# Eight late steps of a tail's down-projection: split float32r products replaced by plain float32 products on two array tiles

## Chip, cores and metric

One Trainium2 chip (trn2), one of its cores. The time is device microseconds of that core, the median of several runs; the trace is one profiled execution.

## What is computed

Block-sparse attention feeds a two-layer feed-forward block. The change touches only the second matrix product of the feed-forward block, `g @ w_out`.

```python
def _attn_ref(q, k, v, sampled_blocks):          # B,H,S,D = 4,8,768,64; blocks of 32
    ...
    return np.matmul(attn, v).astype(np.float32)

def _moe_ref(x, w_in, w_out):                    # x 3072x512, w_in 512x2048, w_out 2048x512
    h = x @ w_in
    g = h * (1.0 / (1.0 + np.exp(-1.702 * h)))
    return (g @ w_out).astype(np.float32)
```

## The kernel before

The 3072 tokens are cut into `NC` = 6 chunks of `CT` = 512 tokens, and the 2048 hidden features into `NF` = 16 groups of 128. A step m = 16 c + f is chunk c and feature group f, so there are 96 steps, 0 to 95. A step has an up product (`h`, 128 features x 512 tokens), a gate (`g`) and a down product, which adds `g`'s 128 features times 128 rows of `w_out` (128 x 512) to four PSUM banks of 128 tokens each.

Every float32 operand of the two products is split into a high part rounded to float32r and a low part (the float32 value minus the high part, again float32r). A product is then three matmuls: high x high, high x low, low x high. For the down product that means, for each step:

- `gate_hi` (line 594, ScalarE) casts `g` to `ghi`, `gate_lo` (line 602, VectorE) subtracts to get `glo`.
- `stream` (line 557) starts a DMA on the SP queue that brings one 256 KB row block of `w_out` from a DRAM scratch tensor into a tile `wst` (pool `work`, two buffers); `split` (line 562 on ScalarE, line 563 on VectorE) makes its high and low part in one of three `wout` buffers.
- `down(m, 0)` issues eight matmuls of 128x128 weights (the tokens of `ghi`) against 512 moving columns (lines 625 and 626: `wout` high, `wout` low, for each of the four banks), and `down(m, 1)` the four of `glo` (line 621). So a step is 12 matmuls over 512 columns.

`slot(d, part)` runs `down(d, part)` and after part 1 `split(d + 2)` and `stream(d + 4)`: weights are fetched four steps ahead and split two steps ahead. [...]

The last two chunks are computed as one block product with fewer multiplications (`pair`, line 837's matmuls), which leaves the gate results of chunk 5 as plain float32 in a resident tile `gs` (16 x 512 columns). The helper tile `snap` (pool `tail`, four buffers) takes copies of PSUM banks there and is last used by the eighth `pair`. After the eighth `pair`, `last` runs steps 78 to 95 with nothing else beside them: for each step of chunk 5 a `gate_hi`, `gate_lo` one step ahead, then the two parts of `slot`. Step 95 is the last of its chunk: it orders its 12 matmuls bank by bank, so that `store` can empty each bank (lines 660 and 662) while the next one is finished.

The attention at the start uses plain float32 matmuls on parts of the array (`tile_position`): the values of the dense blocks (line 419) as two tiles of 128 rows x 64 columns over 65 moving columns, the scores as 64x64 tiles over 384 columns (line 342, four tiles) and as 64x32 tiles over 256 columns (line 332, eight tiles). A call of line 419 issues 24 matmuls in the code, with the two tiles alternating.

Of the kernel before, what the change touches and what calls it, by code (L numbers as in the profile page):

```python
# [9 lines left out]
F32 = mybir.dt.float32  # L10
# [8 lines left out]
P = 128  # L19
# [5 lines left out]
DM = H * D  # L25
DF = 2048
NCT = DM // P
NF = DF // P
NU = (NB - 2) // 2
UT = 2 * BLK  # L30
CU = 8
CT = CU * UT
NC = B * S // CT
NN = CT // P
# [8 lines left out]
MAIN = (NC - TAIL) * NF  # L43
FREEQ = QT * (MAIN - NF) - 10
SPARE = (7, 1, 2, 0)
DV = D + 1
VROW = H * DV
NK = S // P
VDROW = 4 * NK * DV
SV = S + BLK  # L50
# [4 lines left out]
class Kernel:  # L55
# [205 lines left out]
    def load_v(self, e):  # L261
        nc, b, u, r = self.nc, e["b"], e["u"], e["at"]
        if u is None:
            flat = self.vown[r].rearrange("p j c -> p (j c)")[:, 0:VDROW]
            nc.sync.dma_start(out=flat, in_=self.vd[b, e["i"]])
            e["vd"] = flat.rearrange("p (h k a d) -> p h k a d", h=2, a=2, d=DV)
            return
# [126 lines left out]
    def values(self, g):  # L394
# [4 lines left out]
        if g["first"]:  # L399
            un["av"] = self.bank[self.psum("a", un["n"])[0]]  # L400
        sums = un["av"][:, 0:NPAIR * DV].rearrange("p (k d) -> p k d", d=DV)
        if self.sparse(g):
            for i in range(2):
                for h in range(2):
                    for k in range(2):
                        for c in range(4):
                            a, j = c // 2, c % 2
                            at = VROW * (un["b"] % 2) + DV * (2 * (2 * i + a) + h)
                            src = self.vown[r][:, j] if k == j else self.vmid[r]
                            nc.tensor.matmul(  # L410
                                sums[BLK * c:BLK * (c + 1), 2 * i + h], g["pt"][h][:, 2 * i + k, BLK * c:BLK * (c + 1)],
                                src[:, at:at + DV], start=(k == 0), stop=(k == 1), tile_position=(0, BLK * c), skip_group_check=True)
        else:
# [43 lines left out]
    def weights(self):  # L457
# [55 lines left out]
        for k, (f, i) in enumerate(todo):  # L513
            while i == 1 and f - WRING > self.downs - 1:
                yield
            fetch(k + 2)
            if i == 0 and f == NWIN:
                self.opening.close()
                late = self.pool("late", 1)
                self.win += [late.tile([P, 2 * DM], F32R, name=f"win{n}") for n in range(NWIN, NF)]  # L520
            if "a" not in tiles[k]:
                self.flush()
            raw, a = tiles[k]["raw"], tiles[k]["a"]
            nc.vector.tensor_scalar(out=a, in0=a, scalar1=3, scalar2=None, op0=ALU.logical_shift_left)
            yield
            nc.vector.scalar_tensor_tensor(out=a, in0=raw[:, :, 1], scalar=-0x80000000, in1=a, op0=ALU.bitwise_and,
                                           op1=ALU.bitwise_or)
            first(k + 1)
            yield
            if k > 0:  # L530
                if "high" not in tiles[k - 1]:
                    self.flush()
                last(k - 1)
            yield
            nc.vector.scalar_tensor_tensor(out=a, in0=raw[:, :, 0], scalar=29, in1=a, op0=ALU.logical_shift_right,
                                           op1=ALU.bitwise_or)
            tiles[k]["t"] = self.win[f] if i == 0 else self.wout[f % WRING]
            high(k)
            yield
        self.flush()  # L540
        last(len(todo) - 1)

    def flush(self):
# [9 lines left out]
    def stream(self, m):  # L553

        if NF <= m < NC * NF:
            self.wst[m] = self.work.tile([P, DM], F32, name="wst")
            self.nc.sync.dma_start(out=self.wst[m], in_=self.ws[m % NF])

    def split(self, m):
        if m in self.wst:  # L560
            w, t = self.wst.pop(m), self.wout[m % WRING]
            self.nc.scalar.copy(out=t[:, 0:DM], in_=w)  # L562
            self.nc.vector.tensor_tensor(out=t[:, DM:2 * DM], in0=w, in1=t[:, 0:DM].bitcast(F32), op=ALU.subtract)  # L563
# [41 lines left out]
    def down(self, m, part):  # L605
        nc = self.nc
        if m < 0:
            return
        c, f = divmod(m, NF)
        if c == 0:  # L610
            self.need(f, 1)
        _, ghi, glo = self.g[m][-3:]
        w = self.wout[m % WRING]
        woh, wol = w[:, 0:DM], w[:, DM:2 * DM]
        o = [self.bank[3 + n if c < NC - 1 else SPARE[(2, 0, 3, 1)[n]]] for n in range(NN)]
        tk = [slice(n * P, (n + 1) * P) for n in range(NN)]
        last = f == NF - 1
        order = [*range(NN)]

        def low(n):  # L620
            nc.tensor.matmul(o[n], glo[:, tk[n]], woh, start=False, stop=last)  # L621

        if part == 0:
            for n in order:
                nc.tensor.matmul(o[n], ghi[:, tk[n]], woh, start=(f == 0), stop=False)  # L625
                nc.tensor.matmul(o[n], ghi[:, tk[n]], wol, start=False, stop=False)  # L626
                if last:
                    low(n)
            return
        if not last:  # L630
            for n in range(NN):
                low(n)
        del self.g[m]
        self.downs = m + 1
        if last:
            self.store(c, o, order)
# [218 lines left out]
    def pair(self, p):  # L855

        nc = self.nc
        x, z, y = (self.bank[SPARE[n]] for n in (p % 2, 2, 3))
        a11, a12, a22 = self.block(2 * p + 1, 0), self.block(2 * p + 1, 1), self.block(2 * p, 1)
# [50 lines left out]
    def last(self):  # L910
        self.gate_lo(MAIN - 1)
        for p in range(NF // 2):
            self.pair(p)
        end = NC * NF
        for d in range(end - NF - 2, end):
            if end - NF <= d + 1 < end:
                self.g[d + 1] = [self.gs[:, d + 1 - (end - NF)]]
                self.gate_hi(d + 1)
                self.gate_lo(d + 1)
            self.slot(d, 0)  # L920
            self.slot(d, 1)

# [187 lines left out]
```

## Time and profile before

| | before |
|---|---|
| median of 3 runs | 727.82 us (727.42 to 728.03) |
| the profiled execution's own time | 729.48 us |
| its span, first to last instruction | 727.7 us |
| PE (TensorE matmul) busy | 709.0 us (97%), 7554 records |
| PE weight loads busy | 560.9 us (77%) |
| VectorE / ScalarE busy | 450.3 us (62%) / 388.1 us (53%) |
| mean granted TensorE clock | 0.998 of full speed |

[...] The cost of a matmul in a stream is the distance between two starts. A busy PE says only that some matmul is in flight.

### The profile page before, as it was taken

What the parts mean: (1) busy time and instruction counts of PE and PEld (TensorE: products, weight loads), DVE (VectorE), ACT (ScalarE), POOL (GpSimd) and SP (SyncE); (2) the same over time, 40 slices, a digit from 0 to 9 for tenths busy, and PEclk for the clock granted to TensorE, in tenths of its full rate; (3) what the DMA queues carried; (4) which work ended last, traced back from release to release, by engine and by line L of the source; (5) the groups of instructions that cost most, each with busy time, mean ns of one, the idle gap of its engine ahead of it and who ended that gap; (6) DMA issues with size and microseconds to landing.
All of it is one profiled execution on the core that took longest, in us unless ns stands there. A gap on an engine that the chain in (4) does not pass through costs nothing.

```text
span 727.7 us, 18730 instructions
## 1 busy us (share of the span) xinstructions
PE 709.0 (97%) x7554; PEld 560.9 (77%) x7554; DVE 450.3 (62%) x839; ACT 388.1 (53%) x760; POOL 62.5 (9%) x106
## 2 busy tenths in 40 slices
PE   7988999999999999999999999999999999999996
PEld 5656787887777877787778777877778788888885
DVE  5686989898545444454444444544677877676552
ACT  5776777676544544454445445544335554545442
POOL 3254101101100111111001111100000000000000
PEclk9999999999999999999999999999999999999999
DMA  8996877877576665567465545811111311011532
GB/s 349 411 400 228 261 264 247 276 260 259 155 224 198 184 210 176 178 215 224 121 201 170 191 146 178 238 47 43 33 52 35 87 30 45 30 43 30 145 116 72
DMA packets 58568, 123.16 MB, mean 169 GB/s; under 512 B 6961, under 2 KB 24626, under 8 KB 58482
## 3 DMA queue, kind: packets, MB, share of 16 engines
q1 hardware_dynamic: 44768, 76.91, 33.7%
q0 software_dynamic: 6336, 23.43, 9.6%
q10 hardware_dynamic: 7378, 21.63, 8.4%
q8 instruction: 59, 0.97, 0.5%
q14 instruction: 27, 0.22, 0.1%
HBM read 111.46 MB, written 10.49 MB: 168 GB/s over the span
## 4 chain that ended last, share of the span: by engine, by line
PE 83%; DVE 7%; ACT 5%; DMA 3%; issue 1%; ACTq 0%; SPq 0%; DVEq 0%
PE banks L621 11%; PE banks L625 11%; PE banks L626 11%; PE banks L837 10%; PE banks L574 7%; PE banks L575 7%; PE banks L576 7%; PE banks L381 6%; PE banks L410 6%; PE banks L332 5%; DMA raw<-in_moe_w_in_dram 1%; PE banks L443 1%; DVE mx L355 1%; PE banks L419 1%; PE banks L342 1%
## 5 line engine op out<-in xcount | busy, mean ns | idle before, releaser
L625 PE MATMUL banks<-wout,ghi 128*128 128x512 f32 x384 | 151.6, 395 | 0.0
L626 PE MATMUL banks<-wout,ghi 128*128 128x512 f32 x384 | 149.8, 390 | 0.1
L363 ACT ACTIVATE ex<-banks,nm 128x256 f32<-128x256 f32 x176 | 69.0, 478 | 76.1 <-DVE rg L426 53.3
L621 PE MATMUL banks<-wout,glo 128*128 128x512 f32 x384 | 107.6, 395 | 1.2 <-DVE glo L602 1.2
L563 DVE TENSOR_TENSOR wout<-wst,wout 128x512 fp32r<-128x512 f32 x80 | 55.2, 690 | 68.6 <-ACT wout L562 68.0
L582 ACT ACTIVATE g<-banks 128x512 f32<-128x512 f32 x64 | 38.3, 599 | 87.5 <-PE banks L576 87.5
L625 PEld LDWEIGHTS banks<-wout,ghi 128*128 128x128 f32 x384 | 72.1, 188 | 15.9 <-ACT ghi L594 0.4
L621 PEld LDWEIGHTS banks<-wout,glo 128*128 128x128 f32 x384 | 70.7, 188 | 17.4 <-DVE glo L602 2.8
L626 PEld LDWEIGHTS banks<-wout,ghi 128*128 128x128 f32 x384 | 72.2, 188 | 14.9 <-DVE wout L494 0.6
L574 PE MATMUL banks<-x,win 128*128 128x512 f32 x192 | 78.7, 410 | 0.1
L387 ACT COPY pt<-banks 128x512 f32<-128x512 f32 x112 | 61.0, 587 | 27.5 <-PE banks L381 27.1
L575 PE MATMUL banks<-x,win 128*128 128x512 f32 x192 | 75.2, 392 | 0.0
L576 PE MATMUL banks<-x,win 128*128 128x512 f32 x192 | 75.1, 391 | 0.0
L272 POOL DMA_INDIRECT vown<-in_v_dram,vidx x44 | 42.3, 962 | 371.7 <-PE banks L410 359.4
L589 DVE SCALAR_TENSOR_TENSOR g<-g,banks 128x512 f32<-128x512 f32 x51 | 35.0, 687 | 59.1 <-ACT g L582 58.9
L594 ACT CAST ghi<-g 128x512 fp32r<-128x512 f32 x80 | 50.0, 625 | 36.7 <-DVE g L589 30.6
L349 DVE TENSOR_REDUCE mx<-banks 128x4 f32<-128x1024 f32 x44 | 53.7, 1221 | 24.1 <-PE banks L332 24.0
L381 PEld LDWEIGHTS banks<-ident,ex 128*128 128x128 f32 x436 | 49.5, 140 | 15.3 <-ACT pt L387 4.9
L381 PE MATMUL banks<-ident,ex 128*128 128x128 f32 x436 | 58.0, 275 | 2.6 <-ACT pt L387 2.3
L410 PEld LDWEIGHTS banks<-vown,pt 128*32 128x32 f32 x1408 | 42.3, 109 | 19.7 <-issue 15.4
L562 ACT CAST wout<-wst 128x512 fp32r<-128x512 f32 x80 | 50.5, 631 | 9.8 <-DMA wst<-ws 7.9
L602 DVE TENSOR_TENSOR glo<-g,ghi 128x512 fp32r<-128x512 f32 x80 | 54.9, 686 | 0.7
(127 smaller groups left out, 1145.3 us busy)
## 6 DMA issues: line engine op xcount, KB each, us to landing
wst<-ws SPq DMA_DIRECT2D x80, 256.0 KB
kg<-in_kb_dram SPq DMA_DIRECT2D x126, 128.0 KB
raw<-in_moe_w_in_dram ACTq DMA_DIRECT2D x16, 512.0 KB
raw<-in_moe_w_out_dram ACTq DMA_DIRECT2D x16, 512.0 KB
kg<-in_kb_dram SPq DMA_DIRECT2D x18, 384.0 KB
vown<-in_vd_dram SPq DMA_DIRECT2D x8, 780.0 KB
qt<-in_q_dram SPq DMA_DIRECT2D x22, 256.0 KB
out_dram<-ot SPq DMA_DIRECT2D x40, 128.0 KB
```

The lines of the kernel that those rows point to most:

```text
L363: nc.scalar.activation(out=ex[:, cols], in_=sps[h][:, cols], func=AF.Exp, bias=un["nm"][:, c:c + 1], scale=SCALE)
L381: self.nc.tensor.transpose(ps[:, slot], g["ex"][h][:, k * P:(k + 1) * P], self.ident)
L387: self.nc.scalar.copy(out=pt, in_=ps)
L410: nc.tensor.matmul(sums[BLK * c:BLK * (c + 1), 2 * i + h], g["pt"][h][:, 2 * i + k, BLK * c:BLK * (c + 1)], src[:, at:at + DV], start=(k = ...
L563: self.nc.vector.tensor_tensor(out=t[:, DM:2 * DM], in0=w, in1=t[:, 0:DM].bitcast(F32), op=ALU.subtract)
L574: nc.tensor.matmul(h, wih[:, k], hi[:, k], start=(k == 0), stop=False)
L575: nc.tensor.matmul(h, wih[:, k], lo[:, k], start=False, stop=False)
L576: nc.tensor.matmul(h, wil[:, k], hi[:, k], start=False, stop=(k == NCT - 1))
L621: nc.tensor.matmul(o[n], glo[:, tk[n]], woh, start=False, stop=last)
L625: nc.tensor.matmul(o[n], ghi[:, tk[n]], woh, start=(f == 0), stop=False)
L626: nc.tensor.matmul(o[n], ghi[:, tk[n]], wol, start=False, stop=False)
L837: self.nc.tensor.matmul(bank, a[:, k], b[:, k], start=start and k + n == 0, stop=k == 1 and n == 2, skip_group_check=True)
```

## The change

Steps 87 to 94 (`PLAIN`) no longer split anything. Their row block of `w_out` is streamed into a `snap` buffer and stays float32; `split`, `gate_hi` and `gate_lo` are not issued for them. `down` issues for each of the four banks two matmuls, each with 64 tokens of `gs` as weights on one half of the array's columns (`tile_position=(0, 0)` and `(0, 64)`), over the same 512 moving columns, writing partitions 0 to 63 and 64 to 127 of the bank. All eight matmuls of a step stand in part 0; part 1 only drops the tiles. Step 95 is as before.

```diff
--- before.py
+++ after.py
@@ -43,6 +43,7 @@
 MAIN = (NC - TAIL) * NF
 FREEQ = QT * (MAIN - NF) - 10
 SPARE = (7, 1, 2, 0)
+PLAIN = range(NC * NF - 9, NC * NF - 1)
 DV = D + 1
 VROW = H * DV
 NK = S // P
@@ -553,11 +554,11 @@
     def stream(self, m):
 
         if NF <= m < NC * NF:
-            self.wst[m] = self.work.tile([P, DM], F32, name="wst")
+            self.wst[m] = self.tail.tile([P, DM], F32, name="snap", bufs=4) if m in PLAIN else self.work.tile([P, DM], F32, name="wst")
             self.nc.sync.dma_start(out=self.wst[m], in_=self.ws[m % NF])
 
     def split(self, m):
-        if m in self.wst:
+        if m in self.wst and m not in PLAIN:
             w, t = self.wst.pop(m), self.wout[m % WRING]
             self.nc.scalar.copy(out=t[:, 0:DM], in_=w)
             self.nc.vector.tensor_tensor(out=t[:, DM:2 * DM], in0=w, in1=t[:, 0:DM].bitcast(F32), op=ALU.subtract)
@@ -609,12 +610,23 @@
         c, f = divmod(m, NF)
         if c == 0:
             self.need(f, 1)
+        last = f == NF - 1
+        o = [self.bank[3 + n if c < NC - 1 else SPARE[(2, 0, 3, 1)[n]]] for n in range(NN)]
+        if m in PLAIN:
+            if part == 0:
+                for n in range(NN):
+                    for a in range(2):
+                        rows = slice(UT * a, UT * (a + 1))
+                        nc.tensor.matmul(o[n][rows], self.g[m][0][:, n * P + UT * a:n * P + UT * (a + 1)], self.wst[m],
+                                         start=False, stop=False, tile_position=(0, UT * a), skip_group_check=True)
+                return
+            del self.g[m], self.wst[m]
+            self.downs = m + 1
+            return
         _, ghi, glo = self.g[m][-3:]
         w = self.wout[m % WRING]
         woh, wol = w[:, 0:DM], w[:, DM:2 * DM]
-        o = [self.bank[3 + n if c < NC - 1 else SPARE[(2, 0, 3, 1)[n]]] for n in range(NN)]
         tk = [slice(n * P, (n + 1) * P) for n in range(NN)]
-        last = f == NF - 1
         order = [*range(NN)]
 
         def low(n):
@@ -915,8 +927,9 @@
         for d in range(end - NF - 2, end):
             if end - NF <= d + 1 < end:
                 self.g[d + 1] = [self.gs[:, d + 1 - (end - NF)]]
-                self.gate_hi(d + 1)
-                self.gate_lo(d + 1)
+                if d + 1 not in PLAIN:
+                    self.gate_hi(d + 1)
+                    self.gate_lo(d + 1)
             self.slot(d, 0)
             self.slot(d, 1)
 
```

On PE, in the before kernel each of steps 87 to 94 is this sequence; the rows are step 87, taken from PE's order (out<-in, output partitions x moving columns, and the semaphores that it waits for).

```order
L625 MATMUL banks<-wout_120,ghi 128x512 [waits Activation_49]
L626 MATMUL banks<-wout_120,ghi 128x512 [waits DVE_49]
L625 MATMUL banks<-wout_120,ghi 128x512
L626 MATMUL banks<-wout_120,ghi 128x512
L625 MATMUL banks<-wout_120,ghi 128x512
L626 MATMUL banks<-wout_120,ghi 128x512
L625 MATMUL banks<-wout_120,ghi 128x512
L626 MATMUL banks<-wout_120,ghi 128x512
L621 MATMUL banks<-wout_120,glo 128x512 [waits DVE_49]
L621 MATMUL banks<-wout_120,glo 128x512 x3
```

Twelve matmuls with 128 output partitions, which wait for ScalarE's cast and VectorE's two subtractions. In the changed kernel the same place reads as follows, from the end of step 86 to step 90.

```order
L633 MATMUL banks<-wout_122,glo 128x512 x3
L620 MATMUL banks<-snap,gs 64x512 [waits DMAHW7_49]
L620 MATMUL banks<-snap,gs 64x512 x7
L620 MATMUL banks<-snap,gs 64x512 [waits DMAHW0_49]
L620 MATMUL banks<-snap,gs 64x512 x7
L620 MATMUL banks<-snap,gs 64x512 [waits DMAHW1_49]
L620 MATMUL banks<-snap,gs 64x512 x7
L620 MATMUL banks<-snap,gs 64x512 [waits DMAHW2_49]
L620 MATMUL banks<-snap,gs 64x512 x7
```

A step is now eight matmuls with 64 output partitions, and the only wait is for the DMA of its own row block; eight such steps stand between the last `glo` matmul of step 86 and the first `ghi` matmul of step 95.

On the SP queue the loads for steps 86 to 95 read as follows in the changed kernel (`ws_90` to `ws_97` are the row blocks of steps 87 to 94).

```order
L558 DMA wst<-ws_89 128x512 [waits DMAHW6_49,DMAHW4_49,DVE_49]
L558 DMA snap<-ws_90 128x512 [waits DMASW4_49,DMASW5_49,DMASW3_49,DMASW6_49,DMASW2_49,DMASW7_49,DMASW1_49,DMAHW7_49,DMASW0_49,PE_49]
L558 DMA snap<-ws_91 128x512 [waits DMAHW0_49]
L558 DMA snap<-ws_92 128x512 [waits DMAHW1_49]
L558 DMA snap<-ws_93 128x512 [waits DMAHW2_49]
L558 DMA snap<-ws_94 128x512 [waits DMAHW7_49,PE_49]
L558 DMA snap<-ws_95 128x512 [waits DMAHW0_49,PE_49]
L558 DMA snap<-ws_96 128x512 [waits DMAHW5_49,DMAHW1_49,PE_49]
L558 DMA snap<-ws_97 128x512 [waits DMAHW6_49,DMAHW2_49,PE_49]
L558 DMA wst<-ws_98 128x512 [waits DVE_49]
```

Before, all of these waited for VectorE (the `split` that frees a `wst` buffer). Now the loads of steps 91 to 94 wait for PE, that is for the down product four steps earlier, which reads the same `snap` buffer; the load of step 95 stands behind them in the queue.

## Rows read from the trace of the kernel before

**Rows 1.** The page: busy time, granted clock, and the chain that ended last.

```profile
PE 709.0 (97%) x7554; PEld 560.9 (77%) x7554; DVE 450.3 (62%) x839; ACT 388.1 (53%) x760; POOL 62.5 (9%) x106
...
PE 83%; DVE 7%; ACT 5%; DMA 3%; issue 1%; ACTq 0%; SPq 0%; DVEq 0%
```

**Rows 2.** Windows of the tail: length, busy time of each engine, clock, DMA share, GB/s.

```profile
690.00:700.00 10.00, 10.00 (x46) 8.28 (x45) 5.64 (x9) 5.07 (x9) 0.00 (x0) 1.00 0.37 110
700.00:710.00 10.00, 10.00 (x46) 8.28 (x45) 5.17 (x8) 4.38 (x7) 0.00 (x0) 1.00 0.35 102
710.00:720.00 10.00, 10.00 (x46) 8.29 (x45) 3.38 (x6) 3.12 (x5) 0.00 (x0) 1.00 0.09 26
```

**Rows 3.** Timeline, PE: first matmuls of steps 87 and 95 (start, length, engine, instruction).

```profile
697.26 0.39 PE L625 MATMUL banks<-wout,ghi 128*128 128x512 f32 x1
697.48 0.39 PE L626 MATMUL banks<-wout,ghi 128*128 128x512 f32 x1
...
719.02 0.39 PE L625 MATMUL banks<-wout,ghi 128*128 128x512 f32 x1
```

**Rows 4.** Groups of steps 87 to 94 on VectorE and ScalarE: busy, mean ns, idle before.

```profile
L602 DVE TENSOR_TENSOR glo<-gs,ghi 128x512 fp32r<-128x512 f32 x8 | 5.5, 692 | 11.2 <-PE banks L621 11.2
L563 DVE TENSOR_TENSOR wout<-wst,wout 128x512 fp32r<-128x512 f32 x7 | 4.8, 684 | 0.0
L562 ACT CAST wout<-wst 128x512 fp32r<-128x512 f32 x7 | 4.4, 627 | 2.0 <-PE banks L621 2.0
L594 ACT CAST ghi<-gs 128x512 fp32r<-128x512 f32 x7 | 4.4, 624 | 8.3 <-PE banks L626 8.3
```

**Rows 5.** Timeline of the opening, PE: plain float32 stretches on tiles of the array.

```profile
25.35 0.66 PE L381 MATMUL banks<-ident,ex 128*128 128x128 f32 x4
25.93 1.62 PE L419 MATMUL banks<-vown,pt 128*64 128x65 f32 x48
27.48 1.09 PE L332 MATMUL banks<-kg,qt 64*32 64x256 f32 x32
28.51 1.09 PE L381 MATMUL banks<-ident,ex 128*128 128x128 f32 x8
...
36.23 1.52 PE L342 MATMUL banks<-kg,qt 64*64 64x384 f32 x16
37.68 1.09 PE L381 MATMUL banks<-ident,ex 128*128 128x128 f32 x8
```

**Rows 6.** Timeline in windows narrow enough to part one stretch's rounds, PE.

```profile
27.33 0.23 PE L419 MATMUL banks<-vown,pt 128*64 128x65 f32 x2
...
27.48 0.66 PE L332 MATMUL banks<-kg,qt 64*32 64x256 f32 x16
...
27.72 0.64 PE L332 MATMUL banks<-kg,qt 64*32 64x256 f32 x16
...
27.94 0.64 PE L332 MATMUL banks<-kg,qt 64*32 64x256 f32 x16
...
36.60 0.82 PE L342 MATMUL banks<-kg,qt 64*64 64x384 f32 x8
...
36.92 0.83 PE L342 MATMUL banks<-kg,qt 64*64 64x384 f32 x8
```

**Rows 7.** Line 419's records (ns, min/median/max) and its weight loads in the timeline.

```profile
L419 PEld LDWEIGHTS banks<-vown,pt x384: 132/138/139, 14.6 to 59.5; 128*64 128x64 f32 x192
L419 PE MATMUL banks<-vown,pt x384: 217/222/272, 14.6 to 59.6; 128*64 128x65 f32 x192
...
25.93 1.48 PEld L419 LDWEIGHTS banks<-vown,pt 128*64 128x64 f32 x48 [0.17 <-issue]
```

**Rows 8.** Windows of the opening, columns as in rows 2.

```profile
20.00:25.00 5.00, 4.54 (x94) 3.53 (x94) 3.25 (x10) 4.58 (x8) 1.67 (x2) 1.00 1.02 411
25.00:30.00 5.00, 4.92 (x111) 3.75 (x111) 3.26 (x6) 4.44 (x11) 0.00 (x0) 1.00 1.02 412
```

**Rows 9.** Timeline: the first weight load issued in the last stretch, and its waiting reader.

```profile
676.95 4.96 SPq L650 DMA_DIRECT2D out_dram<-ot  x8
...
682.01 28.04 SPq L557 DMA_DIRECT2D wst<-ws  x13
...
684.97 0.62 ACT L562 CAST wout<-wst 128x512 fp32r<-128x512 f32 x1 [4.16 <-DMA wst<-ws]
```

## Prediction

> **What bounds the kernel now.** I read the page first, for the engine that sets the end: PE is busy 97% of the span and carries 83% of the chain of work that ended last [rows 1]. [...] The timeline gives that distance: step 87 starts at 697.26, its second matmul 0.22 later, and step 95 at 719.02 [rows 3]. The eight steps in between take 719.02 - 697.26 = 21.76 us: 2.72 us a step, and over 12 matmuls 0.227 us each.
>
> **What the change takes away.** From PE: 8 x 12 = 96 matmuls, 21.76 us, all of it on the path. From ScalarE and VectorE: two instructions each a step, the cast of `g`, the cast of the weights, and the two subtractions, at 624, 627, 692 and 684 ns [rows 4]. That is 8 x 1.25 = 10.0 us of ScalarE and 8 x 1.38 = 11.0 us of VectorE. I cost this gain at nothing: those engines sat idle waiting for PE (11.2 us ahead of `glo`, 8.3 us ahead of `ghi` [rows 4]), while PE waited for neither [rows 2]. What hides it is the PE stream itself, and that becomes no shorter.
>
> **What it adds.** 8 x 8 = 64 plain float32 matmuls of 128x64 weights over 512 columns. Before has no such row, so I price them from its plain float32 rows on smaller tiles.
>
> *Records.* A call of line 419 issues 24 matmuls and the trace shows 48 records [rows 5], so a plain float32 matmul is two records, and the change makes 128.
>
> *Side by side or not.* The last two records of the line 419 stretch, one for each 128x64 tile, start within 0.01 us (a group of two lasting 0.23 against 0.222 for one record [rows 6, 7]). The stretch has 24 such pairs; the last starts at 27.33, the first at 25.93 [rows 5, 6], so 1.40 / 23 = 0.061 us a pair. The 64 matmuls therefore make 64 pairs of records, if 512 columns behave as 65 do.
>
> *Price of a pair.* It must grow with the columns, and two other shapes show how. A round of the eight 64x32 tiles over 256 columns takes 27.94 - 27.72 = 0.22 us, and a round of the four 64x64 tiles over 384 columns 36.92 - 36.60 = 0.32 us [rows 6]. So 65, 256 and 384 columns cost 0.061, 0.22 and 0.32: near enough to one line, about 0.8 ns a column. By proportion from the nearest row, 0.32 x 512 / 384 = 0.427; I take 0.43 us a pair. The bounds: the line through 65 and 384 columns gives 0.32 + 128 x 0.26 / 319 = 0.424. Taking the whole 384-column stretch, start to next stretch (37.68 - 36.23 = 1.45 us for four rounds [rows 5]), gives 0.363 a round and 0.483 for 512 columns; that loads the cost of entering and leaving onto every round, so it is the upper end. I stay near the lower, since this stretch is 64 rounds long and enters once.
>
> *Entering and leaving.* The array goes from 128x128 tiles to 128x64 and back once. The stretches with tiles cost this much above their rounds, both turns included: 1.45 - 4 x 0.32 = 0.17, and 28.51 - 27.48 - 4 x 0.22 = 0.15 [rows 5, 6]. I take 0.16.
>
> *Weight loads.* 128 of them. Line 419 loads the same 128x64 shape in 138 ns each, and 48 of them stand in 1.48 us [rows 7], where laid end to end they would need 6.6; so they run beside the matmuls even when a pair lasts 0.061 us. At 0.43 I cost them at nothing. [...]
>
> *DMA.* The bytes are the same, and only the waits move: the loads of steps 91 to 94 now wait for the product four steps back, with step 95's load queued behind them and then the output stores. Three steps lie between, 3 x 8 x 0.43 = 10.3 us. A load issued at 682.01, just behind eight output stores, let its reader start at 684.97, 2.96 us later [rows 9]. So I cost this at nothing; without that cover four loads could add up to 3 us each. Step 95's load goes out when step 90 is done, four steps (13.8 us) ahead of its use, and needs 2.96 and then 0.63 and 0.69 us of splitting. The stores after step 95 are as before.
>
> **Sum.** 64 x 0.43 + 0.16 = 27.68 us in place of 21.76: **+5.9 us**. The profiled execution took 729.48 us (span 727.7), by which the changed kernel would take 735.4; its time is 1.7 above the median of the runs, 727.82, and I put the difference on the median: **733.7 us**. With 0.424 it is 733.4; with 0.483, 64 x 0.483 + 0.16 - 21.76 = +9.3, so 737.1.
>
> **Rivals.**
>
> 1. *The weight loads are not hidden.* Each pair waits for its own load: 64 x 0.138 = 8.8 us more, +14.7, 742.5 us. For it: the first pair of a stretch has nothing to hide behind. Against it: the 48 loads in 1.48 us [rows 7].
>
> 2. *The two tiles do not run side by side*, for example because both read the same columns here, which no row of before shows. Then 128 records follow each other: 128 x 0.43 + 0.16 - 21.76 = +33.4, 761.2 us. Against it: pairs that start within 0.01 us on line 419, and four tiles a round on line 342 [rows 5, 6].
>
> [...]
>
> 4. *Faster: a plain float32 record over 512 columns streams as fast as a float32r one.* The doubling would then belong to the short shapes, as a fixed cost or their loads. A pair would take 0.227 us, 64 x 0.227 + 0.16 = 14.7 us, -7.1, so 720.7 us. It decides at a pair of (21.76 - 0.16) / 64 = 0.34 us; below that the change gains. For it: a float32r matmul of the same 512 columns does cost 0.227 [rows 3]. Against it: between 256 and 384 columns the round grows by 0.10 us for 128 columns, already 0.8 ns a column, where float32r pays 0.227 / 512 = 0.44.
>
> **How the numbers follow.** My forecast, with all its bounds, 0.82; rival 1 0.07; rival 2 0.03; rival 3 0.02; rival 4 0.03; and 0.03 for a price between rival 4 and the forecast, two thirds of it within 0.2% (1.5 us, about what a measurement of this kernel can tell from no change) and the rest slower. So faster 0.03, same 0.02, slower 0.95. The forecast alone holds eight in ten, so the range is its own bounds, 733.4 and 737.1, with about 0.7 us below and 0.4 above for the spread of medians (the three runs shown span 0.6): 732.7 to 737.5.
>
> **What would show it.** In the profile after, line 620 should have 128 records in a stretch of about 27.5 us, two starting together, with 0.43 us from pair to pair, clock 1.00, no PE idle time ahead of any of the eight steps, and weight loads starting under the pair before them. ScalarE and VectorE should lose their groups of rows 4 and be idle for most of that stretch. Up to 697 us, and from step 95 to the end, the two traces should agree. [...] PE idle time put down to a `snap` load would show that I was wrong on DMA, and a median below 729 or above 738 that the price of a pair is wrong.

## The result and the profile after

The changed kernel takes **733.9 us** (median of three runs, 733.24 to 734.77) against 727.82: a ratio of 1.0087, 95% interval 1.0067 to 1.0106, so 6.1 us slower. Run again beside the experiments, on another occasion, it took 734.14 against 727.67 (ratio 1.0080, 1.0055 to 1.0105), 6.5 us. The forecast was 733.7, slower.

The page of the changed kernel, the two lines that answer to [rows 1]:

```profile
PE 716.1 (98%) x7586; PEld 552.2 (76%) x7586; DVE 439.4 (60%) x823; ACT 377.6 (52%) x744; POOL 63.1 (9%) x106
...
PE 86%; DVE 5%; DMA 4%; ACT 3%; issue 1%; SPq 0%; ACTq 0%; DVEq 0%
```

VectorE and ScalarE each lost some 11 us of work, and PE gained 7 us and a larger share of the chain. The engine that bounded the tail got the work, and the two that had time to spare gave it up.

The window of the stretch itself, columns as in [rows 2], from the first matmul of step 87 to that of step 95:

```profile
694.91:722.52 27.61, 27.61 (x129) 9.04 (x128) 1.29 (x2) 1.14 (x2) 0.00 (x0) 1.00 0.17 48
```

Eight steps take 27.61 us where they took 21.76 [rows 3]. PE is busy in all of it, the granted clock is 1.00, and VectorE and ScalarE are down to the two instructions each that prepare step 95.

Line 620's records, then the timeline of PE and its weight loads around and in the stretch:

```profile
L620 PEld LDWEIGHTS banks<-snap,gs x128: 132/137/138, 694.9 to 721.6; 128*64 128x64 f32 x128
L620 PE MATMUL banks<-snap,gs x128: 592/592/644, 694.9 to 722.0; 128*64 128x512 f32 x128
```

```profile
693.91 1.07 PE L633 MATMUL banks<-wout,glo 128*128 128x512 f32 x4
...
694.90 0.20 PEld L620 LDWEIGHTS banks<-snap,gs 128*64 128x64 f32 x4 [0.35 <-issue]
694.91 27.69 PE L620 MATMUL banks<-snap,gs 128*64 128x512 f32 x128
695.39 0.14 PEld L620 LDWEIGHTS banks<-snap,gs 128*64 128x64 f32 x2 [0.29 <-issue]
695.82 0.14 PEld L620 LDWEIGHTS banks<-snap,gs 128*64 128x64 f32 x2 [0.29 <-issue]
...
721.57 0.14 PEld L620 LDWEIGHTS banks<-snap,gs 128*64 128x64 f32 x2 [0.29 <-issue]
722.52 0.50 PE L637 MATMUL banks<-wout,ghi 128*128 128x512 f32 x1
...
722.86 0.40 PE L638 MATMUL banks<-wout,ghi 128*128 128x512 f32 x1
```

The matmuls' row merges all 128, but the loads show the rhythm: from the second pair on, two loads at a time stand one pair apart, 61 steps from 695.39 to 721.57, so 26.18 / 61 = **0.429 us a pair**. A record lasts 0.592 us (0.39 in [rows 3], where the next starts 0.22 later), so records overlap, and I read prices from the distance between starts. "Idle, issue" ahead of a load is no loss here: a load of 0.137 us is simply over long before the next is due.

The same place before, from the end of step 86 and at step 95:

```profile
696.35 1.07 PE L621 MATMUL banks<-wout,glo 128*128 128x512 f32 x4
...
719.24 0.39 PE L626 MATMUL banks<-wout,ghi 128*128 128x512 f32 x1
```

**Where the 6 us come from.** I count from the last `glo` matmul of step 86 to the second matmul of step 95, so that both turns of the tile shape are inside. Before: that `glo` matmul started at 697.03 (a group of four from 696.35; the last starts 1.07 - 0.39 = 0.68 later) and step 95's second matmul at 719.24, 22.21 us. After: 693.91 + 0.68 = 694.59 to 722.86, 28.27 us. The difference is 6.06 us, the difference of the medians 6.1. That the two agree so closely is partly chance: the interval of the ratio above, 1.0067 to 1.0106, is 4.9 to 7.7 us.

64 pairs at 0.429 are 27.46 us, 5.70 more than the 21.76 of before; the turns of the tile shape are the other 0.36. They lie in three places: 0.09 ahead of the first pair (694.91 - 694.59 = 0.32 in place of 0.227), 0.15 inside the stretch (27.61 - 27.46), and 0.11 behind step 95's first matmul (722.86 - 722.52 = 0.34 in place of 0.227).

The two profiled spans (727.7 and 731.4) differ by only 3.7. The rest lies ahead of the change, where the changed kernel is already 2.44 us early (694.59 against 697.03). The first up product of these two executions starts at 72.78 and 69.91, 2.87 us apart with the same code up to there; 0.43 of that is lost again by the end of step 86.

```profile
72.78 0.50 PE L574 MATMUL banks<-x,win 128*128 128x512 f32 x1
```

```profile
69.91 0.50 PE L575 MATMUL banks<-x,win 128*128 128x512 f32 x1
```

The first row is of the kernel before, the second of the changed one. In the repeated run of the changed kernel the same matmul starts at 71.9. The opening ends some microseconds earlier or later from execution to execution, and a difference of 6 us must not be read from two spans; read it from the stretch.

### The profile page after: what moved, and what is told of

It reads as the page before. It is cut to its first block, busy times and chain, and to the rows that moved or that the text cites. A ratio compares the mean times of both kernels' runs of the same rounds, so it can differ in the third digit from the quotient of the medians.

```text
span 731.4 us, 18736 instructions
## 1 busy us (share of the span) xinstructions
PE 716.1 (98%) x7586; PEld 552.2 (76%) x7586; DVE 439.4 (60%) x823; ACT 377.6 (52%) x744; POOL 63.1 (9%) x106
## 4 chain that ended last, share of the span: by engine, by line
PE 86%; DVE 5%; DMA 4%; ACT 3%; issue 1%; SPq 0%; ACTq 0%; DVEq 0%
PE banks L633 10%; PE banks L637 10%; PE banks L638 10%; PE banks L849 10%; PE banks L575 8%; PE banks L576 7%; PE banks L577 7%; PE banks L333 6%; PE banks L382 6%; PE banks L411 6%; PE banks L620 4%; DMA raw<-in_moe_w_in_dram 2%; PE banks L444 1%; PE banks L420 1%; PE banks L343 1%; DVE gs L772 1%
## 5 line engine op out<-in xcount | busy, mean ns | idle before, releaser
L637 PE MATMUL banks<-wout,ghi 128*128 128x512 f32 x352 | 139.1, 395 | 0.0
L638 PE MATMUL banks<-wout,ghi 128*128 128x512 f32 x352 | 137.3, 390 | 0.6 <-DVE wout L495 0.6
L564 DVE TENSOR_TENSOR wout<-wst,wout 128x512 fp32r<-128x512 f32 x72 | 49.7, 691 | 90.1 <-ACT wout L563 87.8
L633 PE MATMUL banks<-wout,glo 128*128 128x512 f32 x352 | 99.1, 395 | 1.2 <-DVE glo L603 1.0
L637 PEld LDWEIGHTS banks<-wout,ghi 128*128 128x128 f32 x352 | 66.1, 188 | 15.3 <-issue 0.8
L633 PEld LDWEIGHTS banks<-wout,glo 128*128 128x128 f32 x352 | 64.7, 188 | 16.1 <-DVE glo L603 2.8
L638 PEld LDWEIGHTS banks<-wout,ghi 128*128 128x128 f32 x352 | 66.1, 188 | 14.2 <-DVE wout L495 1.0
L563 ACT CAST wout<-wst 128x512 fp32r<-128x512 f32 x72 | 45.5, 631 | 29.0 <-DMA wst<-ws 29.0
```

## The experiments

The theory: the tail costs what its records cost, 64 pairs at 0.429 us, plus some 0.35 us for the two turns; the second tile of a pair is free; the work taken off the other engines is worth nothing. The rivals: the tiles are not really side by side or gain something over a full-width product; the split work beside the matmuls had a cost; the loss is mostly the turns.

The experiments were run in two groups and one more alone. Beside the first group the kernel before took 727.67 us (19 runs), beside the second, on another chip, 730.27 (13 runs); each experiment is set against the runs beside it.

### The changed kernel again

> The changed kernel once more, beside the others on one chip: 733.9 us within 0.7, the stretch of 128 records 27.6 us long, pairs 0.429 us apart.

Measured: 734.14 us (733.89 to 735.13), the stretch again 27.6 us.

### One full-width product in place of two half-width ones

```diff
-                    for a in range(2):
-                        rows = slice(UT * a, UT * (a + 1))
-                        nc.tensor.matmul(o[n][rows], self.g[m][0][:, n * P + UT * a:n * P + UT * (a + 1)], self.wst[m], ...)
+                    nc.tensor.matmul(o[n], self.g[m][0][:, n * P:(n + 1) * P], self.wst[m], ...)
```

> As the changed kernel, but the plain float32 products of steps 87 to 94 use the whole array: four matmuls of 128x128 weights a step in place of eight of 128x64. [...] Rival: the side-by-side tiles are what keeps the plain product from being dearer, the full-width one takes 0.85 us a record, the stretch 55 us, the time 761 us.

Measured: 732.95 us (732.89 to 733.64), ratio 1.0068 (1.0042 to 1.0093). PE's timeline:

```profile
694.82 27.63 PE L618 MATMUL banks<-snap,gs 128*128 128x512 f32 x64
721.88 0.79 PE L634 MATMUL banks<-wout,ghi 128*128 128x512 f32 x1
722.52 0.40 PE L635 MATMUL banks<-wout,ghi 128*128 128x512 f32 x1
```

64 records of the whole array, 0.43 us each, half of the rival's 0.85: the same length as 64 pairs of half-width records. So the side-by-side tiles gain nothing that a plain full-width product doesn't have; they only make two records of one. From the first plain record to step 95's second matmul it is 27.70 us here and 27.95 with tiles; with the entry it is 0.34 less, about the price of the turns. (Step 95's first matmul is recorded here as early as 721.88 and as 0.79 us long, so I compare second ones.) The medians are 1.2 apart, but the intervals of the two ratios overlap.

### The split work left out, the matmuls kept

```diff
-        if NF <= m < NC * NF:
+        if NF <= m < NC * NF and m not in PLAIN:
...
-        _, ghi, glo = self.g[m][-3:]
-        w = self.wout[m % WRING]
+        if m not in PLAIN:
+            self.parted = self.g[m][-2:]
+        ghi, glo = self.parted
+        w = self.wout[(PLAIN[0] - 1 if m in PLAIN else m) % WRING]
...
-                self.gate_hi(d + 1)
-                self.gate_lo(d + 1)
+                if d + 1 not in PLAIN:
+                    self.gate_hi(d + 1)
+                    self.gate_lo(d + 1)
```

> The kernel before, with ScalarE's, VectorE's and the DMA's work for steps 87 to 94 left out (no weight load, no split of the weights, no split of the gate; the 96 matmuls stay and read the parts of step 86). My theory: what the change took off ScalarE and VectorE was hidden, so the time is that of the kernel before, 727.8 us within 0.7. [...]

Measured: 729.46 us, ratio 1.0021 (1.0010 to 1.0032): slower than expected. Its waits and its timeline show that this is the experiment's own doing:

```profile
ACT wout L563 <- PE banks L624: 24.8, 1, 24.8
DVE wout L564 <- ACT wout L563: 24.4, 1, 24.4
...
PE banks L628 <- ACT wout L563: 0.7, 1, 0.7
```

```profile
712.54 1.07 PE L624 MATMUL banks<-wout,glo 128*128 128x512 f32 x4
713.65 0.62 ACT L563 CAST wout<-wst 128x512 fp32r<-128x512 f32 x1 [24.76 <-PE banks L624]
714.32 0.49 PE L628 MATMUL banks<-wout,ghi 128*128 128x512 f32 x1 [0.71 <-ACT wout L563]
...
717.67 0.39 PE L628 MATMUL banks<-wout,ghi 128*128 128x512 f32 x1
```

All eight steps read the `wout` buffer that step 95's split has to write, and that split stands between steps 93 and 94 in the program. So it waited 24.8 us for the last matmul of step 93 (the `glo` group at 712.54), and step 94, which reads the same buffer, waited for it. Step 94 starts 1.10 us behind the matmul before it (713.22 to 714.32) in place of 0.227 and lasts 3.35 (to 717.67) in place of 2.72: 1.5 us together, which is the ratio's loss. With the buffer of step 85 read instead (`PLAIN[0] - 2`), that is gone:

> As e3_no_split_work, but the 96 matmuls of steps 87 to 94 read the weight parts of step 85, so that the split for step 95 finds its buffer free. Again no weight load, no split of the weights and no split of the gate for the eight steps. My theory: the stretch is 21.76 us as in the kernel before and the time 727.7 us within 0.7. [...]

Measured: 730.22 us against 730.27 in its group, ratio 1.0002 (0.9991 to 1.0013). A window of its tail, and the first matmuls of steps 87 and 95:

```profile
700.00:710.00 10.00, 10.00 (x46) 8.28 (x45) 0.00 (x0) 0.00 (x0) 0.00 (x0) 1.00 0.00 0
```

```profile
697.58 0.39 PE L628 MATMUL banks<-wout,ghi 128*128 128x512 f32 x1
...
719.34 0.39 PE L628 MATMUL banks<-wout,ghi 128*128 128x512 f32 x1
```

In this window VectorE, ScalarE and the DMA do nothing at all, and PE issues the same 46 matmuls in the 10 us as in [rows 2]; the stretch is 719.34 - 697.58 = 21.76 us to the hundredth. What the change takes off those engines is worth nothing, and the distance of 0.227 us between float32r matmuls is the same without that work beside them.

### Four steps, and four steps apart

```diff
-PLAIN = range(NC * NF - 9, NC * NF - 1)
+PLAIN = range(NC * NF - 5, NC * NF - 1)
```

> As the changed kernel, with only the last four of the eight steps (91 to 94) plain. My theory: a step costs 8 pairs x 0.429 = 3.43 us in place of 2.72, so 0.71 more, and the two turns of the tile shape cost 0.35 once: 4 x 0.71 + 0.35 = +3.2, 731.0 us. Rival: the loss is mostly a cost of entering and leaving, then it stays near +6, 733.9 us.

Measured: 731.41 us (729.79 to 733.39, ten runs), ratio 1.0047 (1.0032 to 1.0061), +3.4 us by the ratio.

```profile
708.01 13.95 PE L620 MATMUL banks<-snap,gs 128*64 128x512 f32 x64
721.90 0.50 PE L637 MATMUL banks<-wout,ghi 128*128 128x512 f32 x1
```

The four steps last 13.89 us in place of 4 x 2.72 = 10.88: 3.01 more, and 3.2 with the 0.09 and 0.11 of the turns that lie outside these two rows. So the loss grows with the steps.

```diff
-PLAIN = range(NC * NF - 9, NC * NF - 1)
+PLAIN = range(NC * NF - 9, NC * NF - 1, 2)
```

> As the changed kernel, with steps 87, 89, 91 and 93 plain and the ones between them split: four plain steps as in e4_four_steps, but eight turns of the tile shape in place of two. My theory: each way in and out costs about 0.35 us together (0.09 before the first pair, 0.05 for the first pair, 0.10 and 0.11 after the last), so the time is four steps of 0.71 and four visits of 0.35 above the kernel before, +4.2, 731.9 us, with 25.9 us from the start of step 87 to that of step 95. Rival: a turn costs nothing by itself, then +2.9, 730.6 us, and 24.6 us.

Measured: 735.12 us against 730.27, ratio 1.0069 (1.0044 to 1.0094); that is 3.2 to 6.9 us, so the trace has to tell. PE's timeline of the first visit and of step 95:

```profile
700.54 3.65 PE L620 MATMUL banks<-snap,gs 128*64 128x512 f32 x16
704.13 0.50 PE L637 MATMUL banks<-wout,ghi 128*128 128x512 f32 x1
704.47 0.40 PE L638 MATMUL banks<-wout,ghi 128*128 128x512 f32 x1
...
726.56 0.39 PE L637 MATMUL banks<-wout,ghi 128*128 128x512 f32 x1
```

From step 87 to step 95 it is 26.02 us, 4.26 above the kernel before (25.9 us was expected). With the 0.09 of the first entry, which lies outside, 4.35, against 3.2 for the same four plain steps in a row: three more visits cost some 1.14 us, **0.38 each**. One sees where: a pair takes 0.429, but from the last pair's start (700.54 + 3.65 - 0.59 = 703.60) to the next float32r matmul it is 0.53, and from that one to its neighbour 704.47 - 704.13 = 0.34 instead of 0.227.

### One tile alone

```diff
-                    for a in range(2):
+                    for a in range(1):
```

> As the changed kernel, but only the left tile's matmuls: the right half of the tokens of steps 87 to 94 is left out, 32 matmuls and 64 records in place of 64 and 128. My theory: the second tile of a pair costs nothing, so 64 single records at 0.429 us take as long as 64 pairs, the stretch stays 27.5 us and the time 734 us. Rival: the tiles share the array's time, and half of the work takes half of the stretch, 13.9 us, 720 us.

Measured: 738.1 us in one run, in the group where the kernel before takes 730.27. Line 620 in this run:

```profile
L620 PEld LDWEIGHTS banks<-snap,gs x64: 133/137/137, 699.8 to 726.4; 128*64 128x64 f32 x64
L620 PE MATMUL banks<-snap,gs x64: 592/592/644, 699.8 to 726.9; 128*64 128x512 f32 x64
```

Half of the records, the same 27 us from first to last start (the changed kernel: 694.9 to 722.0). The second tile of a pair is free. The one run lies 7.8 us above the kernel before, 1.7 more than the changed kernel does; what makes up that difference was not looked for, and I go by the stretch.

### The tiles' matmuls in another order

```diff
-                for n in range(NN):
-                    for a in range(2):
+                for a in range(2):
+                    for n in range(NN):
```

> As the changed kernel, with the eight matmuls of a plain step in another order: the four banks' matmuls of the left tile first, then the four of the right tile. My theory: PE starts matmuls in the order of the program, so two records run side by side only where neighbours in the order lie on different tiles; a step then has 16 records with an overlap only at the change of tile, 14 to 16 starts of 0.429 us, 6.0 to 6.9 us a step, and the time is 754 to 761 us. Rival: PE looks ahead and starts the other tile's matmuls early, whatever the order; then pairs stay 0.429 us apart and the time stays at 734 us.

Measured: 739.3 us in one run. Neither theory holds. The stretch, the next record of PE, then its weight loads in the timeline and one DMA:

```profile
698.39 30.25 PE L620 MATMUL banks<-snap,gs 128*64 128x512 f32 x128
728.56 0.50 PE L637 MATMUL banks<-wout,ghi 128*128 128x512 f32 x1
...
698.38 0.19 PEld L620 LDWEIGHTS banks<-snap,gs 128*64 128x64 f32 x2 [0.35 <-issue]
698.87 0.14 PEld L620 LDWEIGHTS banks<-snap,gs 128*64 128x64 f32 x1 [0.29 <-issue]
699.30 0.14 PEld L620 LDWEIGHTS banks<-snap,gs 128*64 128x64 f32 x1 [0.29 <-issue]
699.73 0.14 PEld L620 LDWEIGHTS banks<-snap,gs 128*64 128x64 f32 x1 [0.29 <-issue]
700.16 0.19 PEld L620 LDWEIGHTS banks<-snap,gs 128*64 128x64 f32 x3 [0.29 <-issue]
700.59 0.19 PEld L620 LDWEIGHTS banks<-snap,gs 128*64 128x64 f32 x2 [0.24 <-issue]
...
701.93 0.19 PEld L620 LDWEIGHTS banks<-snap,gs 128*64 128x64 f32 x3 [0.29 <-issue]
...
703.84 0.32 SPq L558 DMA_DIRECT2D snap<-ws  x1
```

The left tile runs alone for four records; with its fifth, at 700.16, the right tile starts, although its first matmul stands behind the left one's eighth record. From there on the tiles run beside each other, the right one four records late, so only four records at either end are alone. The views do not name a record's tile; I read it from the order in the code. The semaphores bear it out at the next change of tile. In the trace the load that waits for step 88's row block is one of the three at 701.93, when 13 of step 87's 16 records have started; step 87's last record, which signals its end, starts only three pairs later, at 703.22, and the DMA that waits for that signal goes out at 703.84. So step 88's first record starts ahead of three records of step 87. If that lead of four is fixed, the 15 changes of tile overlap four records each: 128 - 15 x 4 = 68 starts, 29.2 us, and some 0.06 at each change makes 30.1. The stretch is 30.2 us (698.39 to 728.56).

Whether the lead is fixed was tested with two steps of one tile ahead of two of the other:

```diff
-                for n in range(NN):
-                    for a in range(2):
+                for a in range(2):
+                    for s in (m, m + 1) if (m - PLAIN[0]) % 2 == 0 else ():
+                        for n in range(NN):
...
```

> As e1_tile_by_tile, with two steps' left-tile matmuls (8 matmuls, 16 records) ahead of the same two steps' right-tile ones. In e1 the right tile's first record started together with the fifth of the left tile's eight, so it had been let past some of them. Theory one: a tile's record may start a fixed four records ahead of its turn; then each change of tile overlaps four records, the 128 records need 128 - 7 x 4 = 100 starts of 0.429 us, and the stretch is 43 us. Theory two: it may be let past as many as stand in the way after some first ones; then the right tile starts 12 records late at most and stays beside the left one, 76 starts, 32.6 us, plus some 0.06 at each change. If PE kept to the order of the program, the stretch would be near 52 us.

Measured: 751.93 us in one run, with 730.36 for the kernel before beside it.

```profile
697.81 43.53 PE L621 MATMUL banks<-snap,gs 128*64 128x512 f32 x128
741.27 0.50 PE L638 MATMUL banks<-wout,ghi 128*128 128x512 f32 x1
```

741.27 - 697.81 = 43.5 us: theory one, 100 starts. Program order alone would have needed about 52, and a lead that grows with need 33.

## Why the prediction was right

**The bound and the hidden gain.** The prediction costed 10 us of ScalarE and 11 us of VectorE at nothing because PE waited for neither: by [rows 2] PE's stream has no gap there, so its matmuls set the tail's length. Shown: with that work left out and the matmuls kept, the stretch is 21.76 us as before.

**The price of a pair.** Predicted 0.43 from rounds of 256 and 384 columns [rows 6], measured 0.429. The bound of 0.483 was too high for the reason that the prediction gave, a turn spread over only four rounds. The extension to 512 columns held, and with it the rejection of rival 4: a plain record pays 0.429 / 512 = 0.84 ns a column.

**Side by side.** Predicted from line 419's pairs; shown by the one-tile run, in which half of the work takes the same 27 us. That both tiles read the same columns did no harm (0.429 us a pair), so rival 2 is out. The prediction assumed no more than that neighbours in the order overlap, and the code alternates the tiles; the order runs show that it matters (stretches of 30.2 and 43.5 us against 27.6).

**Weight loads.** Predicted hidden; 128 loads of 0.137 us cost nothing beside pairs of 0.429 (the one-tile run has half of the loads and the same 27 us); from the second pair on, a pair's two matmuls and the two loads for the next pair start together (695.39), so rival 1 is out.

**Entering and leaving.** The one term that was mis-sized: 0.16, measured 28.27 - 22.21 - (64 x 0.429 - 21.76) = 0.36, and 0.38 a visit in the every-other run. The 0.16 was taken from the first record of a tiled stretch to the first of the next stretch [rows 5, 6], and by that measure it holds: 0.15 here. What the measure leaves out is the delay on either side of it, 0.09 ahead of the first pair and 0.11 behind the first matmul after the last. Whether the opening's turns have these two as well was not looked at.

**DMA.** Predicted at nothing, with 10.3 us of cover. The SP queue's timeline and step 95's cast:

```profile
698.60 10.62 SPq L558 DMA_DIRECT2D snap<-ws  x4
...
709.27 0.42 SPq L558 DMA_DIRECT2D wst<-ws  x1
...
712.16 0.62 ACT L563 CAST wout<-wst 128x512 fp32r<-128x512 f32 x1 [22.87 <-DMA wst<-ws]
```

The four loads that wait for PE go out as steps 87 to 90 end. Step 95's follows at 709.27 and lets its reader start at 712.16, 2.89 us later and 10 us ahead of step 95. The 22.87 us are ScalarE's idle time, which cost nothing: PE was busy in all 27.61 us of the stretch.

**Clock.** The granted clock was 1.00 through the stretch; the 0.02 of rival 3 stood for a lower one, which no run here shows (means of 0.996 to 1.000).

**The sum.** +5.9 predicted, +6.06 in the stretch, +6.1 in the medians. The two errors, 0.2 too little for the turns and some 0.06 too much for the 64 pairs, are small beside the interval of the measurement, so that 733.7 and 733.9 lie 0.2 apart is partly luck; the price of a pair, read from the stretch, is not. What the prediction expected of the trace ahead of the change, that both would agree up to 697 us, did not hold: the opening alone was 2.87 us shorter in this execution.

No version that beats the kernel before came out of this: every plain step costs 0.7 us more, with tiles or without.

## What to carry to other kernels

Weigh such an exchange on the bounding engine alone: three float32r matmuls at 0.227 us (0.68) against a plain float32 product at two records of 0.429 (0.86), full width or as two half-width tiles that run side by side. The work that it took off idle engines was no gain here (ratio 1.0002 with that work left out); a plain step could pay only where PE waits for the splitting, by more than 0.7 us a step here, and that was not tried. Price an unseen shape from two or three sizes of the same kind in the trace, and read a difference of a few microseconds from the stretch, not from two spans.

## What was not expected of the hardware

In the two runs with another order, matmuls on different tiles did not start in the order of the program: the other tile's record started four records ahead of its turn, no sooner, in two layouts (a stretch of 30.2 us with runs of 8 records, 43.5 with runs of 16; 27.6 alternating). In the first of them step 88's first record started at 701.93, step 87's last at 703.22. What sets the four is open.

A float32r matmul of 512 columns cost 0.227 us here, 0.44 ns a column, and a plain record on the same columns 0.429, less than twice that. The 0.227 was the same without the work on the other engines; what sets either price was not tried.
